# Grouped attention into a routed MoE: one transfer for a unit's q, one for its k, heads paired by two, five matmuls ahead of the first transposes, and q ahead of k in the first unit

## The chip, the cores and the metric

The kernel is one program on 1 core of a Trainium2 chip. The metric is device time in microseconds for one execution. A few runs are timed; their median stands for the kernel, and one further execution is taken with the hardware profiler, whose rows are quoted below.

## The reference

Attention is computed in chunks of 64 positions inside each head, with no mixing between chunks. Its output is the input of a mixture of experts in which a token keeps the expert of the token before it unless a gate says otherwise.

```python
B, H, S, D = 8, 8, 576, 64            # q, k, v: (B, H, S, D), float32
nc = S // 64
scores = scale * np.matmul(q_c, k_c.transpose(0, 1, 2, 4, 3))   # per 64-row chunk
attn = np.exp(scores - max); attn = attn / (sum + 1e-09)
out = np.matmul(attn, v_c)
...
x = out.transpose(0, 2, 1, 3).reshape(B, S, H * D)               # 512 columns, head after head
e = argmax(logits[b, s]) if s == 0 or local_gate[b, s] < 0.5 else prev_e
h = np.maximum(x[b, s] @ w1[e], 0.0)                             # 512 -> 1024
out[b, s] = p[e] * (h @ w2[e])                                   # 1024 -> 512
```

## The kernel before, in words

The 4608 rows (8 batches of 576) are cut into 18 units of 256 rows, numbered 0 to 17. A unit is 256 neighbouring rows of one batch, except units 6 and 15, whose rows are the last 64 of four batches ("mixed rows"). `load_qk(i)` fills two buffers of 512 KB, `qt` and `kt`, from a ring of six pairs (three of them are `lenth`/`lentl`, space that the weights take later). For a plain unit each of q and k comes in two transfers of 256 KB: partition 4p+g holds eight consecutive rows of head g in its first half (transfer j=0) and of head g+4 in its second half (j=1). For mixed rows each comes in four transfers of 128 KB. `load_v(i)` brings v, two transfers of 256 KB whose runs are 256 bytes long.

All transfers are issued from SyncE's queue (SP) in program order, the first unit's k excepted, which ScalarE's queue issues. There are eight completion semaphores for them, taken in turn, so a transfer waits for the one eight places ahead of it; SP also waits where the data queue takes no more.

A unit then passes these steps:
- `pair_heads`: four copies of 128x512 into `qr` and `kr` put heads side by side (`p0` = "AVPA" says which engines do it for unit 0: ScalarE, VectorE, GpSimd, ScalarE; later units all on GpSimd). Each copy reads both halves of `qt` or `kt`. `qr` and `kr` have one buffer each.
- `qk_transposes`: eight 128x128 transposes on TensorE for q and eight for k, in groups of four, each group copied out of PSUM to `qT` or `kT`.
- `scores`: 32 small matmuls into `sc`; row maxima, subtraction and exponential follow (`mx`, `pr`).
- `p_transposes`, then `values`: 32 matmuls with v into `o`, and a division by the row sum into `xs` (`norm`, one call for each half j of the heads).
- `x_transposes`, `router`: the logits; the unit's rows then go to `x_d` in DRAM.

The order on TensorE, VectorE, ScalarE and GpSimd is written out by hand: `PAR["start"]` for the first units (tokens such as `p0` pair, `t0a`..`t0d` the four groups of transposes, `s0` scores), `PAR["steady"]` for one iteration of the loop over units. In iteration i the loop handles scores of unit i+1, transposes of q and k of unit i+2, pairing of unit i+3, q and k loads of unit i+5 and v loads of unit i+2, beside the values of unit i-1 and the router of unit i-2. In the first unit four transposes of unit 1 (`t1a`) stand ahead of the scores of unit 0 (`s0`).

After the attention the rows are routed, gathered from `x_d` tile by tile and multiplied by the experts' weights; that is the rest of the program, and the change does not touch it.

The lines that set the heads' places in `values`, which stay for the units that are not changed:

```python
pT[64 * cc:64 * cc + 64, 4 * j + h, 64 * cp:64 * cp + 64],
vt[cp][64 * cc:64 * cc + 64, 4 * j + h, 0:D + 1],
```

Of the kernel before, what the change touches and what calls it, by code (L numbers as in the profile page):

```python
# [8 lines left out]
F32 = mybir.dt.float32  # L9
# [11 lines left out]
B, H, S, D = 8, 8, 576, 64  # L21
E, F = 8, 1024
C = H * D
N = B * S
P = 128
NT = N // P
NS = N // 256
# [50 lines left out]
def tile_attention_then_moe(ctx: ExitStack, tc, q, k, v, wg, wl, w1, w2, out):  # L78
    nc = tc.nc
# [7 lines left out]
    def ENG(x):  # L87
        return tuple({"A": nc.scalar, "V": nc.vector, "P": nc.gpsimd}[c] for c in x)

    ident = cpool.tile([P, P], F32, name="ident")  # L90
# [29 lines left out]
    ps_tr = ctx.enter_context(tc.tile_pool(name="ps_tr", bufs=3, space=PSUM))  # L120
# [7 lines left out]
    for i in range(2):  # L128
        vt = pa1.tile([P, VS], F32, name=f"v{i}")[:, 0:2 * H * DW].rearrange("p (c h d) -> p c h d", c=2, d=DW)
# [4 lines left out]
    def place(i):  # L134
        ph, j = divmod(i, 9)
        if j == LEFT:
            return 9 * ph + 8, [(4 * ph + n, 512, 64) for n in range(4)]
        j -= j > LEFT
        return 9 * ph + j, [(4 * ph + j // 2, 256 * (j % 2), 256)]

    def mixed_rows(i):
        return i % 9 == LEFT

    def load_qk(i):
        qt, kt = qkbuf[i % len(qkbuf)]
        for m, (b, s0, n) in enumerate(place(i)[1]):
            for dst, src in ((qt, q), (kt, k)):
                if mixed_rows(i):
                    nc.sync.dma_start(
                        dst[m::4].rearrange("p (h n) -> p h n", h=H),  # L150
                        src[b, :, s0:s0 + n, :].rearrange("h (p r) d -> p h (r d)", r=2))
                    continue
                for j in range(2):
                    (nc.scalar if i == 0 and src is k else nc.sync).dma_start(
                        dst[:, 8 * D * j:8 * D * j + 8 * D],
                        src[b, 4 * j:4 * j + 4, s0:s0 + n, :].rearrange("g (p r) d -> p g (r d)", r=8))
        return qt, kt
# [112 lines left out]
        return atoms  # L270


    def values(pT, vt, xs, fine=False):
        box = {}

        def group(j, h):
            if h == 0:
                box["o"] = ps_o.tile([P, 2, 512], F32, name="o")
            o = box["o"]
            for cp in range(2):  # L280
                for cc in range(2):
                    nc.tensor.matmul(
                        o[64 * cp:64 * cp + 64, cc, DV * h:DV * h + D + 1],
                        pT[64 * cc:64 * cc + 64, 4 * j + h, 64 * cp:64 * cp + 64],
                        vt[cp][64 * cc:64 * cc + 64, 4 * j + h, 0:D + 1],
                        start=True, stop=True,
                    )
            if h == 3 and not fine:
                norm(j)

        def norm(j):
                ov = box["o"][:, :, 0:4 * DV].rearrange("p c (h d) -> p c h d", d=DV)
                rs = pa2.tile([P, 2, 4], F32, name="rs")
                nc.vector.tensor_scalar_add(rs, ov[:, :, :, D], 1e-9)
                nc.vector.reciprocal(rs, rs)
                nc.vector.tensor_tensor(
                    xs[:, :, 256 * j:256 * j + 256].rearrange("p c (h d) -> p c h d", d=D),
                    ov[:, :, :, 0:D],
                    rs.unsqueeze(3).to_broadcast([P, 2, 4, D]),
                    ALU.mult,  # L300
                )

        out = []
        for j in range(2):
            out += [lambda j=j, h=h: group(j, h) for h in range(4)]
            if fine:
                out.append(lambda j=j: norm(j))
        return out
# [185 lines left out]
    qk, hd, vts, qkT, prs, pTs, xss, xTs = ({} for _ in range(8))  # L494

    def a_tq(i, engs=None):
        qkT[i] = (pe2.tile([P, 4, 256], F32, name="qT", bufs=1), pe2.tile([P, 4, 256], F32, name="kT", bufs=1))
        return qk_transposes(i, hd.pop(i), *qkT[i], engs)

    def a_pair(i, engs=(nc.gpsimd,) * 4):  # L500
        hd[i], fns = pair_heads(i, qk.pop(i), engs)
        return fns

    def a_sa(i, fine=False):
        prs[i] = pa2.tile([P, H, 2, D], F32, name="pr")
        return scores(*qkT.pop(i), prs[i], fine)

    def a_tp(i, fine=False):
        pTs[i] = pa2.tile([P, H, P], F32, name="pT")
        return p_transposes(prs.pop(i), pTs[i], fine)  # L510
# [3 lines left out]
    def a_va(i, fine=False):  # L514
        if not rows:
            rows.extend(pa2.tile([P, XS], F32, name=f"xs{n}", bufs=1) for n in range(NX))
        xss[i] = rows[i % NX][:, 0:2 * XR].rearrange("p (c n) -> p c n", c=2)
        if i < NX:
            nc.gpsimd.memset(xss[i][:, :, XL:XR], 0.0)
        return values(pTs.pop(i), vts.pop(i), xss[i], fine)  # L520

    def a_tx(i, fine=False):
        xTs[i] = pa2.tile([P, 4, 256], F32, name="xT", bufs=1)
# [5 lines left out]
    def play(order, qs):  # L529
        its = {}  # L530
        for tok in order.split():
            name, _, n = tok.partition("*")
            if name not in its:
                its[name] = iter(qs[name]())
            for _ in range(int(n or 1)):
                next(its[name])()
        for name, it in its.items():
            assert next(it, None) is None, name
        assert set(its) == set(qs), set(qs) - set(its)
# [54 lines left out]
    with tc.manual_schedule(engines=MAN | {ET.Pool}):  # L594
        warm = pa2.tile([P, 1], F32, name="warm", tag="xT", bufs=1)
        nc.scalar.activation(warm, ident[:, 0:1], AF.Exp)

        def load(store, fn, i):
            def go():
                store[i] = fn(i)  # L600
            return lambda: [go]

        tqs = {}

        def tq(i, g):
            if i not in tqs:
                tqs[i] = a_tq(i, ENG(PAR[f"t{i}"]))
            return tqs[i][5 * g:5 * g + 5]

        st = {f"p{i}": lambda i=i: a_pair(i, ENG(PAR[f"p{i}"])) for i in range(4)}  # L610
        st |= dict(
            s0=lambda: a_sa(0, True), q3=load(qk, load_qk, 3),
            s1=lambda: a_sa(1, True), o0=lambda: a_tp(0, True), q4=load(qk, load_qk, 4), q5=load(qk, load_qk, 5),
            v2=load(vts, load_v, 2))
        for i in range(3):
            for g in range(4):
                st[f"t{i}{'abcd'[g]}"] = lambda i=i, g=g: tq(i, g)
        st |= dict(wg=lambda: [lambda: (
            nc.sync.dma_start(wg9[:, :, 0:8], wg.rearrange("(c p) e -> p c e", p=P)),
            nc.sync.dma_start(wg9[:, :, 8:9], wl.rearrange("(c p) e -> p c e", p=P)))])  # L620
        play(PAR["start"], st)
# [247 lines left out]
    for i in range(1, NS - 2):  # L869
# [12 lines left out]
        if 8 <= i < 16:  # L882
            c, col = divmod(i - 8, 2)
# [13 lines left out]
    n = NS - 1  # L897
# [356 lines left out]
```

## Time and profile before

| | |
|---|---|
| median of 3 runs | 638.35 us (638.34 to 639.34) |
| profiled execution, its own time | 638.56 us |
| span from the first to the last instruction in it | 636.8 us |
| around the span | 1.76 us |
| TensorE (PE) busy | 608.1 us, 96% of the span |
| VectorE (DVE), ScalarE (ACT), GpSimd (POOL) busy | 380.3, 255.8, 147.0 us |
| moved by transfers | 97.83 MB, mean 154 GB/s |

A busy PE is not a PE at its peak: its matmuls are pipelined, their ends are modelled, and a pause of PE can lie inside a matmul's modelled time. All times within the execution count from the first instruction of the span. The first 160 us are the attention units, in which the transfers are dense; afterwards PE works on the experts.

### The profile page before, as it was taken

Reading aid. Unit: us, or ns where it says so; the run is one execution under the profiler, and the core shown is the slowest. Engines: PE = TensorE matmul, PEld = TensorE weight load, DVE = VectorE, ACT = ScalarE, POOL = GpSimd, SP = SyncE. Lnnn points to the kernel's source line nnn. Section 1 sums busy time; section 2 is a strip of 40 time slices with the busy share of each in tenths; the row PEclk is TensorE's granted clock in tenths of the full one; section 3 lists DMA queues with packets and bytes.
Section 4 is the critical chain, followed back from the end, with each engine's and each line's share of the span. In section 5 each row is a group of like instructions: output and inputs, shape, how many; then the busy total and the mean of one; then the engine's idle time right before and its main releaser. Section 6 shows DMA issues by size and latency. Waiting matters only on the chain. (4 is left out here: it accounts for less than half of the span.)

```text
span 636.8 us, 17170 instructions
## 1 busy us (share of the span) xinstructions
PE 608.1 (96%) x5904; PEld 513.6 (81%) x5904; DVE 380.3 (60%) x990; ACT 255.8 (40%) x468; POOL 147.0 (23%) x219
## 2 busy tenths in 40 slices
PE   4899989889999999999999999999999999999995
PEld 4788777777779788789998996789888998788884
DVE  2677678887795667575434556763478533387231
ACT  4677667664421252532112443421465211343120
POOL 3353244550050302021021021031021221010201
PEclk9999999999999999999999999999999999999999
DMA  8999999998440245155021264452086511054111
GB/s 267 264 265 301 284 272 264 303 286 271 158 150 21 71 151 185 44 178 180 20 70 55 61 206 134 151 178 64 27 271 203 190 52 59 30 184 147 65 30 36
DMA packets 78355, 97.83 MB, mean 154 GB/s; under 512 B 42672, under 2 KB 46768, under 8 KB 78192
## 3 DMA queue, kind: packets, MB, share of 16 engines
q1 hardware_dynamic: 71744, 75.30, 37.9%
q0 software_dynamic: 6160, 19.99, 9.6%
q8 instruction: 84, 1.38, 0.9%
q14 instruction: 79, 0.65, 0.3%
q10 hardware_dynamic: 288, 0.52, 0.3%
HBM read 76.62 MB, written 19.69 MB: 151 GB/s over the span
## 5 line engine op out<-in xcount | busy, mean ns | idle before, releaser
L804 POOL DMA_INDIRECT out<-ysb,sidx x38 | 40.2, 1058 | 356.3 <-DVEq L1028 160.6
L743 PE MATMUL y<-w2h,hq 128*128 128x512 f32 x368 | 119.8, 395 | 1.3 <-DVE ysb L1078 1.0
L743 PEld LDWEIGHTS y<-w2h,hq 128*128 128x128 f32 x368 | 69.1, 188 | 16.9 <-issue 2.5
L743 PE MATMUL y<-w2l,hq 128*128 128x512 f32 x184 | 71.9, 391 | 0.0
L1050 PE MATMUL tr<-xp,w1h 128*128 128x256 f32 x528 | 67.0, 283 | 0.0
L1050 PEld LDWEIGHTS tr<-xp,w1h 128*128 128x128 f32 x528 | 65.5, 192 | 1.2 <-ACT w2h L1011 0.4
L743 PE MATMUL y<-w2h,hp 128*128 128x512 f32 x192 | 63.3, 397 | 0.3 <-ACT hp L690 0.3
L722 PE MATMUL h<-w1h,xp 128*128 128x512 f32 x208 | 60.5, 396 | 0.0
L1058 ACT ACTIVATE hq<-tr 128x256 fp32r<-128x256 f32 x51 | 18.9, 383 | 68.4 <-PE tr L1050 44.8
L1078 DVE TENSOR_SCALAR ysb<-y,ppr 128x512 f32<-128x512 f32 x33 | 24.8, 751 | 34.4 <-PE y L743 30.3
L722 PEld LDWEIGHTS h<-w1h,xp 128*128 128x128 f32 x208 | 38.1, 188 | 7.4
L694 POOL DMA_INDIRECT xg<-x_d,gidx x36 | 38.5, 1069 | 19.8 <-issue 14.5
L743 PEld LDWEIGHTS y<-w2h,hp 128*128 128x128 f32 x192 | 36.0, 188 | 8.1 <-ACT hp L690 0.5
L789 ACT ACTIVATE hsb<-h 128x512 f32<-128x512 f32 x26 | 14.1, 596 | 66.1 <-PE h L722 49.1
L1059 DVE SCALAR_TENSOR_TENSOR hq<-tr,hq 128x256 fp32r<-128x256 f32 x51 | 21.1, 423 | 32.3 <-ACT hq L1058 28.6
L743 PEld LDWEIGHTS y<-w2l,hq 128*128 128x128 f32 x184 | 34.6, 188 | 6.9 <-DVEq L1028 0.3
L743 PE MATMUL y<-w2l,hp 128*128 128x512 f32 x96 | 37.5, 390 | 0.0
L1018 DVE TENSOR_TENSOR w1l<-raw,w1h 128x1024 fp32r<-128x1024 f32 x28 | 32.4, 1221 | 8.3 <-ACT w1h L1011 4.9
L691 DVE TENSOR_TENSOR xp<-tr,xp 128x512 fp32r<-128x512 f32 x39 | 25.5, 686 | 18.6 <-ACT xp L690 15.8
L1050 PE MATMUL tr<-xp,w1l 128*128 128x256 f32 x264 | 35.3, 283 | 0.0
L1018 DVE TENSOR_TENSOR w2l<-raw,w2h 128x1024 fp32r<-128x1024 f32 x28 | 32.8, 1223 | 1.2 <-issue 1.2
L1050 PEld LDWEIGHTS tr<-xp,w1l 128*128 128x128 f32 x264 | 33.3, 192 | 0.0
(242 smaller groups left out, 1152.7 us busy)
## 6 DMA issues: line engine op xcount, KB each, us to landing
raw<-in_moe_w SPq DMA_DIRECT2D x72, 512.0 KB
x_d<-xs SPq DMA_DIRECT2D x16, 528.0 KB
v<-in_v SPq DMA_DIRECT2D x20, 256.0 KB
qt<-in_q SPq DMA_DIRECT2D x16, 256.0 KB
lenth<-in_q SPq DMA_DIRECT2D x16, 256.0 KB
lentl<-in_k SPq DMA_DIRECT2D x16, 256.0 KB
kt<-in_k SPq DMA_DIRECT2D x14, 256.0 KB
raw<-in_v SPq DMA_DIRECT2D x6, 256.0 KB
```

Of the source, the lines that this page charges most:

```text
L691: lambda: V.tensor_tensor(lo, box["ps"], hi.bitcast(F32), ALU.subtract)]
L694: nc.gpsimd.indirect_dma_start(out=dst, out_offset=None, in_=src, in_offset=bass.IndirectOffsetOnAxis(ap=gidx[t].bitcast(U32), axis=0))
L722: nc.tensor.matmul(hs[:, j], xs[a][:, c], W1[w][c][:, 512 * j:512 * j + 512], start=(c == 0 and n == 0), stop=(c == 3 and n == 2))
L743: nc.tensor.matmul(y, h_of(t, f // 4)[a][:, f % 4], W2[w][c][:, f % 2, :], start=(f == 0 and n == 0), stop=(f == 7 and n == 2))
L789: nc.scalar.activation(hsb[:, 512 * j:512 * j + 512], hs[:, j], AF.Relu)
L804: nc.gpsimd.indirect_dma_start(out=out, out_offset=bass.IndirectOffsetOnAxis(ap=sidx[t].bitcast(U32), axis=0), in_=ysb, in_offset=None, bo ...
L1018: V.tensor_tensor(lo[c], raw[c], hi[c].bitcast(F32), ALU.subtract)
L1050: nc.tensor.matmul(hb[:, 256 * n:256 * n + 256], W1[w][c][:, P * (f + n):P * (f + n) + P], XP[:, x, c].rearrange("p s t -> p (s t)"), star ...
L1058: nc.scalar.activation(hi, ps, AF.Relu)
L1059: V.scalar_tensor_tensor(lo, ps, 0.0, hi.bitcast(F32), ALU.max, ALU.subtract)
L1078: V.tensor_scalar(ysb, y, pr, None, ALU.mult)
```

## The change

Four things are changed.

1. For units 1 to 15 without the mixed ones (13 units) q comes in one transfer of 512 KB and k in another. A partition then holds heads 2g and 2g+1 where it held g and g+4.
2. `values` follows: for those units head 2h+j of v goes with place 4j+h of the scores, and `norm` writes its half of the heads to every second block of 64 columns of `xs`.
3. In unit 0, SP and ScalarE's queue each issue one half of q first, and then one half of k.
4. Five matmuls on the identity matrix, 256 columns each, stand first on PE. Nothing reads their result.

```diff
+    def heads_by_two(i):
+        return 0 < i < NS - 2 and not mixed_rows(i)
...
+                if heads_by_two(i):
+                    nc.sync.dma_start(
+                        dst.rearrange("p (j n) -> p j n", j=2),
+                        src[b, :, s0:s0 + n, :].rearrange("h (p r) d -> p h (r d)", r=8))
+                    continue
                 for j in range(2):
-                    (nc.scalar if i == 0 and src is k else nc.sync).dma_start(
+                    (nc.scalar if i == 0 and j == 1 else nc.sync).dma_start(
...
+        if by_two:
+            xv = xs[:, :, 0:C].rearrange("p c (h j d) -> p j c h d", j=2, d=D)
+        else:
+            xv = xs[:, :, 0:C].rearrange("p c (j h d) -> p j c h d", j=2, d=D)
...
-                        vt[cp][64 * cc:64 * cc + 64, 4 * j + h, 0:D + 1],
+                        vt[cp][64 * cc:64 * cc + 64, 2 * h + j if by_two else 4 * j + h, 0:D + 1],
...
-                    xs[:, :, 256 * j:256 * j + 256].rearrange("p c (h d) -> p c h d", d=D),
+                    xv[:, j],
...
+        awake = ps_tr.tile([P, 4, P], F32, name="tr")
+        for _ in range(5):
+            nc.tensor.matmul(awake[:, 0:2], ident, ident.unsqueeze(1).to_broadcast([P, 2, P]), start=True, stop=True)
```

On SP's queue the program begins with these transfers before (`qt_120` and `kt_121` are unit 0's, the next two unit 1's, the next two unit 2's; `v_126` and `v_127` are v of units 0 and 1):

```order
L154 DMA qt_120<-in_q 128x1x512 x2
L154 DMA qt_122<-in_q 128x1x512 x2
L154 DMA kt_123<-in_k 128x1x512 x2
L165 DMA v_126<-in_v 128x8x64 x2
L154 DMA qt_124<-in_q 128x1x512 x2
L154 DMA kt_125<-in_k 128x1x512 x2
L165 DMA v_127<-in_v 128x8x64 x2
```

and with these of the change:

```order
L162 DMA qt_120<-in_q 128x1x512
L162 DMA kt_121<-in_k 128x1x512
L157 DMA qt_122<-in_q 128x2x512
L157 DMA kt_123<-in_k 128x2x512
L173 DMA v_126<-in_v 128x8x64 x2
L157 DMA qt_124<-in_q 128x2x512
L157 DMA kt_125<-in_k 128x2x512
L173 DMA v_127<-in_v 128x8x64 x2
```

From unit 1 on a pair of rows has become one row with twice the elements, and a half of unit 0's k has come in from ScalarE's queue, to which a half of its q went. On ScalarE's queue the start was this before (`warm` loads the exponential's table, `qr` and `kr` are the pairing copies):

```order
L154 DMA kt_121<-in_k 128x1x512 x2
L596 ACT_TABLE_LOAD
L596 ACTIVATE warm<-ident 128x1
L188 COPY qr<-qt_120 128x4x128
L188 COPY kr<-kt_121 128x4x128
```

and is this with the change:

```order
L162 DMA qt_120<-in_q 128x1x512
L162 DMA kt_121<-in_k 128x1x512
L608 ACT_TABLE_LOAD
L608 ACTIVATE warm<-ident 128x1
L196 COPY qr<-qt_120 128x4x128
L196 COPY kr<-kt_121 128x4x128
```

Only the two transfers differ. On PE the program begins so before (`tr<-ident,qr` are transposes of q, `sc` the scores of unit 0):

```order
L198 MATMUL tr<-ident,qr 128x128 x8
L198 MATMUL tr<-ident,kr 128x128 x8
L198 MATMUL tr<-ident,qr 128x128 x4
L233 MATMUL sc<-kT,qT 64x64 x32
L198 MATMUL tr<-ident,qr 128x128 x4
```

and so with the change:

```order
L611 MATMUL tr<-ident 128x256 x5
L206 MATMUL tr<-ident,qr 128x128 x8
L206 MATMUL tr<-ident,kr 128x128 x8
L206 MATMUL tr<-ident,qr 128x128 x4
L241 MATMUL sc<-kT,qT 64x64 x32
L206 MATMUL tr<-ident,qr 128x128 x4
```

The five matmuls stand ahead of all else; nothing behind them has moved.

## Rows read from the trace of the kernel before

**Rows 1.** The page: busy us of each engine, share of the span, instructions.
```profile
PE 608.1 (96%) x5904; PEld 513.6 (81%) x5904; DVE 380.3 (60%) x990; ACT 255.8 (40%) x468; POOL 147.0 (23%) x219
```

**Rows 2.** By the microsecond: busy us (instructions) by engine, granted clock, DMA share, GB/s.
```profile
2.00:3.00 1.00, 0.00 (x0) 0.00 (x0) 0.00 (x0) 0.94 (x1) 0.00 (x0) 1.00 0.59 131
3.00:4.00 1.00, 0.00 (x0) 0.00 (x0) 0.00 (x0) 0.55 (x2) 0.00 (x0) 1.00 1.04 354
4.00:5.00 1.00, 0.00 (x0) 0.00 (x0) 0.00 (x0) 0.00 (x0) 0.00 (x0) 1.00 1.07 412
5.00:6.00 1.00, 0.00 (x0) 0.00 (x0) 0.00 (x0) 0.00 (x0) 0.41 (x1) 1.00 1.02 393
6.00:7.00 1.00, 0.06 (x1) 0.09 (x2) 0.43 (x1) 0.82 (x2) 0.24 (x2) 1.00 1.06 404
```

**Rows 3.** Timeline from 0 to 40 us: start, duration, engine, line, operation, idle before.
```profile
1.43 0.28 POOL masks.py:199 TENSOR_SCALAR_AFFINE_SELECT ident<-ident 128x128 f32<-128x128 f32 x1
...
5.59 0.61 POOL L190 COPY kr<-kt 128x512 f32<-128x512 f32 x1 [3.87 <-DMA kt<-in_k]
...
6.18 0.62 ACT L188 COPY qr<-qt 128x512 f32<-128x512 f32 x1 [2.62 <-DMA qt<-in_q]
```

**Rows 4.** Timeline of PE from 5 to 32 us.
```profile
6.95 1.94 PE L198 MATMUL tr<-ident,qr 128*128 128x128 f32 x8 [6.95 <-ACT qr L188]
8.68 1.92 PE L198 MATMUL tr<-ident,kr 128*128 128x128 f32 x8
10.38 1.05 PE L198 MATMUL tr<-ident,qr 128*128 128x128 f32 x4
11.37 1.16 PE L233 MATMUL sc<-kT,qT 64*64 64x64 f32 x64
...
16.32 1.09 PE L198 MATMUL tr<-ident,qr 128*128 128x128 f32 x8
17.25 1.16 PE L198 MATMUL tr<-ident,pr 128*128 128x128 f32 x8
18.36 1.06 PE L198 MATMUL tr<-ident,kr 128*128 128x128 f32 x8
20.75 1.16 PE L233 MATMUL sc<-kT,qT 64*64 64x64 f32 x64 [1.33 <-ACT pr L252]
...
22.31 1.09 PE L198 MATMUL tr<-ident,qr 128*128 128x128 f32 x8
```

**Rows 5.** Timeline of PE around the first 512-column float32 matmuls in the experts.
```profile
257.12 3.65 PE L737 MATMUL m<-raw,fullx 128*64 128x512 f32 x16
```

**Rows 6.** Timeline from 0 to 40 us, GpSimd's pairing copies of units 2 and 3.
```profile
15.01 1.17 POOL L190 COPY kr<-kt 128x512 f32<-128x512 f32 x2 [0.60 <-DMA kt<-in_k]
...
18.96 1.17 POOL L190 COPY qr<-lenth 128x512 f32<-128x512 f32 x2 [2.78 <-DMA lenth<-in_q]
```

**Rows 7.** Waits of PE from 28 to 140 us: total us, times, longest.
```profile
PE sc L233 <- issue: 3.4, 5, 1.4
PE o L282 <- issue: 2.0, 2, 1.3
```

**Rows 8.** Timeline of PE from 40 to 80 us: the scores of unit 8.
```profile
64.89 0.58 PE L233 MATMUL sc<-kT,qT 64*64 64x64 f32 x24 [1.44 <-issue]
```

**Rows 9.** SP's timeline: k of unit 2, q of unit 3, v of unit 12.
```profile
9.22 1.25 SPq L154 DMA_DIRECT2D kt<-in_k  x2
...
12.06 3.34 SPq L154 DMA_DIRECT2D lenth<-in_q  x2
...
106.03 1.27 SPq L165 DMA_DIRECT2D v<-in_v  x2
```

**Rows 10.** Timeline of PE from 110 to 113 us: the values of unit 12.
```profile
111.87 0.65 PE L282 MATMUL o<-v,pT 64*64 64x65 f32 x32
```

**Rows 11.** Groups of VectorE from 0 to 150 us: line, op, count, busy us, mean ns.
```profile
L296 DVE TENSOR_TENSOR xs<-o,rs 128x512 f32<-128x512 f32 x33 | 22.8, 691 | 1.1
```

**Rows 12.** Transfer queues from 0 to 140 us: packets, MB, share.
```profile
q8 instruction: 22, 0.36, 1.0%
```

More of the change, by code (lines that the diff above doesn't have):

```diff
@@ L270, in p_transposes, with values @@
         return atoms
-    def values(pT, vt, xs, fine=False):
+    def values(pT, vt, xs, fine=False, by_two=False):
         box = {}
+        if by_two:
+            xv = xs[:, :, 0:C].rearrange("p c (h j d) -> p j c h d", j=2, d=D)
+        else:
+            xv = xs[:, :, 0:C].rearrange("p c (j h d) -> p j c h d", j=2, d=D)
         def group(j, h):
@@ L519, in a_va @@
             nc.gpsimd.memset(xss[i][:, :, XL:XR], 0.0)
-        return values(pTs.pop(i), vts.pop(i), xss[i], fine)
+        return values(pTs.pop(i), vts.pop(i), xss[i], fine, heads_by_two(i))
     def a_tx(i, fine=False):
```

## The prediction

> **What bounds the kernel now.** I read the page first, then the stretches, the timeline from the start, and last the waits. PE is busy for 608.1 us of the span of 636.8 [rows 1], so a gain must either start PE's work sooner or close one of its pauses. The chain that ended last does not reach back far enough to help: it covers only the tail of the program. So I follow PE from its first instruction. It does nothing for 6.95 us; its first transposes then wait for ScalarE's pairing copy of q [rows 4], and that copy was released by a transfer of q, at 6.18 [rows 3]. GpSimd's copy of k, released by k's transfers, started at 5.59 [rows 3]: k was there before q, though PE needs q first.
>
> The second thing is PE's speed. Eight transposes of q and eight of k run from 6.95 to 10.38 [rows 4], 0.214 us each. From 16.32 to 17.25 eight of the same shape take 0.93 us, 0.116 each [rows 4]. These are the two levels, 1.2 and 2.4 GHz. The granted clock reads 1.00 even in the stretch where PE starts [rows 2], so it has no record of the low level, and the spacing must tell. The slow spacing lasts until the scores at 11.37, which take 1.16 like later ones, at 20.75 for one [rows 4]: PE ran slow for 4.4 us after its first matmul and was at 2.4 GHz then.
>
> The third is who waits for transfers. After the first unit, rows say so only of GpSimd's copies: k of unit 2 at 15.01, q of unit 3 at 18.96 [rows 6], and a little for k of unit 3. PE's own pauses between 28 and 140 us are put down to "issue": 3.4 us before scores and 2.0 before values, in 7 pauses of up to 1.4 [rows 7]. So in the steady part the transfers are full but PE is fed; what is saved at the start should stay saved, as long as the transfers keep ahead.
>
> **The change, part by part.**
>
> *q ahead of k.* The data moved by 4.0 us is 131 + 354 = 0.485 MB; by 5.0 it is 0.897, by 6.0 1.290 and by 7.0 1.694 [rows 2]. The first pair of transfers (0.524 MB) is in at 4.1, the second (1.049 MB) at 5.4. Before, q's second half was the last of these four, and its copies began 0.8 after 5.4. With the change both halves of q are first on their queues, so its copies should begin at 4.1 + 0.8 = 4.9, 1.3 earlier; the copy on ScalarE takes 0.62 [rows 3], and q would be ready for PE at 5.65 (before, PE's 6.95 came 0.77 after 6.18). k is now last of the four: its copies begin at 6.2, 0.6 later than GpSimd's did, and with 0.62 each are done at 6.85. Unit 1's q is in when 1.573 MB have moved, 6.7, and can be copied from 7.5.
>
> *Five matmuls.* They need only the identity, which is done at 1.71 [rows 3], so they start near 1.8. No row shows this shape. The nearest are float32 matmuls of 512 columns, sixteen records side by side in pairs in 3.65 us [rows 5]: 0.43 to 0.46 for a pair at 2.4 GHz, so 0.22 for 256 columns, and a float32 matmul is two such records (the 32 of `scores` stand as x64 in a row). That is 0.44 each, 0.88 at 1.2 GHz: 4.4 us in all if slow, 2.2 if fast. PE is then free between 4.0 and 6.2. I take the slow end, since in the one stretch that tells, every matmul with less than 4.4 us of work behind it was slow. The first transposes then start at 6.2 instead of 6.95; the five matmuls cost about half a microsecond here, because q is ready at 5.65.
>
> *The clock.* 4.4 us after 1.8 is 6.2: if PE behaves as in its own first stretch, it is at 2.4 GHz when the transposes of q begin. They end at 7.15; those of k, ready at 6.85, follow until 8.1. Before, the scores started 0.99 after the end of k's transposes (8.68 to 10.38, then 11.37, with the copy to `kT` between) [rows 4]. With the change that gives 9.1. The four transposes of unit 1 that stand ahead of the scores need GpSimd's two copies, 1.17 [rows 6] from 7.5, so 8.67, and 0.47 of PE: 9.15. **Scores of unit 0 at 9.15 instead of 11.37: 2.2 us earlier.**
>
> *What the next units allow.* If their data comes no sooner than before, two places cap the gain. k of unit 2: GpSimd starts at 15.01, takes 1.17, and PE uses it at 18.36: 2.18 of slack. q of unit 3: 18.96 + 1.17 = 20.13 against 22.31: 2.18 again [rows 4, 6]. So 2.2 just fits.
>
> *One transfer for two.* Two transfers of 256 KB cost SP 1.25 us where it is not held up [rows 9]; one should cost half, since neither the bytes nor the runs (2 KB on the DRAM side) change. That frees 1.25 us of SP a unit. It hides behind the transfers themselves, which already move 354 to 412 GB/s from 3 us on [rows 2], and behind holds of SP like the 2.1 us in its 3.34 for q of unit 3 [rows 9], so I count 0. If the cover were gone, it would bring v, which stands behind k on SP, up to 1.25 us forward. A copy reads both halves of its buffer anyway, so nothing waits longer for a whole unit.
>
> *The heads' new places.* PE's matmuls only read other columns. `norm` writes blocks of 64 columns with gaps instead of 256 in a row, 13 units of 2 writes. They take 691 ns now [rows 11]. No row has the gapped form; from 0 to a doubling (0.7 us each) it would lie on VectorE, which is 60% busy, so 0 and no range of its own.
>
> The sum is made against the profiled execution: 638.56 - 2.2 = **636.4 us**. Its own time is 0.2 above the median of the runs, 638.35; I leave the number there. Differences under 0.2%, 1.3 us, are not told from no change here, so faster means under 637.1.
>
> **The rivals.**
>
> *The clock is late.* If the five matmuls don't bring PE to 2.4 GHz by the time the transposes start, or it falls back while only transposes run, 20 transposes cost 0.098 more each, 2.0 us; scores come near 10.9 and the gain is 0.5 (up to 1.2 if the clock comes in the middle). For: one stretch alone shows when it rises. Against: in that stretch nothing but transposes ran, and the scores that followed were fast. Time 637.8, chance 0.15. The Trainium skill has a rule of this kind: "TensorE: Matmul & The Clock Gate", Part 4, says that transposes do not count as work for the clock. By that rule the clock would not have risen before the scores at 11.37, and it had [rows 4]; so this trace does not bear it out.
>
> *The transfers set the pace later.* PE's lead of 2.2 us must be there at every unit. The tightest place I find is v of unit 12: SP has issued it by 107.30 [rows 9] and PE reads it at 111.87 [rows 10], 4.6 later. Where an engine did wait, the data came 4.5 after the end of the issue (k of unit 2: 10.47 to 15.01) and 3.6 (q of unit 3: 15.40 to 18.96) [rows 6, 9]. That leaves 0.1 to 1.0 us for v if SP keeps its times. It should not, having 1.25 us more a unit. If that helps nothing, the gain falls to about 1.0. Time 637.5, chance 0.15.
>
> *Slower, by the supply of instructions.* PE paused at 64.89 for 1.44 us in the middle of one group of 64 records [rows 8], where no data is waited for. Instruction packets, 22 in 140 us of 16 KB each [rows 12], share the transfer engines. Twice the bytes per request, issued sooner, may keep these engines fuller and such packets later. To turn the gain into a loss of 1.3 takes 3.5 us more: from 7 pauses [rows 7] to 10, at 1.2 each. At four more of 1.4: 636.4 + 5.6 = 642. For: the pauses exist only where transfers are dense. Against: the bytes are the same. The five matmuls also move the places where packets end by some twenty instructions, which can lose pauses as well as win them. Chance 0.10.
>
> *More than forecast.* The same shift takes away a pause or two (1.4 each), or the clock rises while the five matmuls run: 635.0. Chance 0.12.
>
> **How the numbers follow.** The forecast has 0.48: gains of 1.5 to 2.7, 635.9 to 637.0. Faster by over 0.2%: 0.48 + 0.12 + 0.03 of the two smaller gains = 0.63. Within 0.2%: 0.27. Slower: 0.10. For 8 in 10 I leave out the slower case and the better half of the best: 635.0 to 638.1.
>
> **What would show it.** In the profile after: copies of q on ScalarE and VectorE released by a transfer near 4.9 (right) or near 6 (q was not first in fact); PE's first row at 1.8, ending near 6.2; eight transposes of q in 0.93 us and not 1.7; scores of unit 0 near 9.15; q of unit 3 used near 20.1 on PE. Then the distance to the times of before should stay near 2.2 at 55, 110 and 160 us. If it shrinks with a wait on v, the transfers were the bound; if it jumps at rows with "issue", it was instructions. The forecast is wrong if the transposes stay slow, if a merged transfer lands later than its two halves did, or if pauses of PE change by more than 2 us in sum.

## The result, and the profile after

The changed kernel took 647.64 us (644.42 to 649.72, 4 runs) against 638.85 us (638.34 to 640.41, 4 runs) of the kernel before on the same chips: 1.0122 times as long, 95% interval 1.0097 to 1.0147. It is slower by 1.2%, about 8 us. Ratios in this text leave out executions more than 1.5% above the fastest of their kernel: two of late_merged (649.82 and 649.13), one each of after_again and merged_dummy. The forecast was 636.4, with 635.0 to 638.1 as its range; the case that came true was its rival of 0.10, the supply of instructions. A second measurement of the same kernel later gave 1.0101 (1.0066 to 1.0136).

The profiled execution took 644.42 us, with a span of 642.6, so it is one of the quicker ones. PE has 3.9 us more busy time than in [rows 1]; the five matmuls alone take 4.5:

```profile
PE 612.0 (95%) x5914; PEld 515.2 (80%) x5914; DVE 383.0 (60%) x990; ACT 255.8 (40%) x468; POOL 146.9 (23%) x219
```

**The start did most of what was forecast.** The timeline of the first 13 us (start, duration, engine, line, operation, idle before):

```profile
0.74 0.66 ACTq L162 DMA_DIRECT2D qt<-in_q  x1
...
1.77 4.54 PE L611 MATMUL tr<-ident 128*128 128x256 f32 x10 [1.77 <-POOL ident masks.py:199]
...
4.71 0.62 ACT L196 COPY qr<-qt 128x512 f32<-128x512 f32 x1 [1.14 <-DMA qt<-in_q]
...
6.16 1.04 PE L206 MATMUL tr<-ident,qr 128*128 128x128 f32 x8
...
7.03 1.23 PE L206 MATMUL tr<-ident,kr 128*128 128x128 f32 x8
...
8.86 1.16 POOL L198 COPY qr<-qt 128x512 f32<-128x512 f32 x2 [2.00 <-DMA qt<-in_q]
9.52 0.66 PE L206 MATMUL tr<-ident,qr 128*128 128x128 f32 x4 [1.26 <-POOL qr L198]
10.11 1.16 PE L241 MATMUL sc<-kT,qT 64*64 64x64 f32 x64
```

The copy of q starts at 4.71 (forecast 4.9). The five matmuls hold PE from 1.77 to 6.16. The eight transposes of q then take 0.87 us, from 6.16 to 7.03, where eight took 1.73 before [rows 4]: PE is at 2.4 GHz here, from the first transpose on (not so in every execution, see "Why the prediction was wrong"). But PE then waits 1.26 us for GpSimd's copy of unit 1's q, and that waited for its transfer: it can start at 8.86, not at 7.5. How much of this is the merging is not shown: the copy needs both halves in either form, and in the kernels with q first it starts between 7.55 (merged_dummy) and 9.50 us (no_awake) where unit 1's q is merged, between 7.34 (v_first_halves) and 8.37 (v_first_start) where it is not. The transfers as a sum are a little behind too (by the microsecond: busy us of PE, PEld, DVE, ACT, POOL, granted clock, DMA share, GB/s):

```profile
2.00:3.00 1.00, 1.00 (x3) 0.82 (x4) 0.00 (x0) 0.93 (x1) 0.00 (x0) 1.00 0.65 180
3.00:4.00 1.00, 1.00 (x3) 0.80 (x3) 0.00 (x0) 0.56 (x2) 0.00 (x0) 1.00 1.00 379
4.00:5.00 1.00, 1.00 (x4) 0.75 (x3) 0.28 (x1) 0.29 (x1) 0.00 (x0) 1.00 1.04 361
5.00:6.00 1.00, 1.00 (x4) 0.82 (x3) 0.15 (x1) 0.33 (x1) 0.00 (x0) 1.00 0.93 311
6.00:7.00 1.00, 1.00 (x9) 0.85 (x9) 0.21 (x1) 0.62 (x1) 0.66 (x2) 1.00 1.00 356
```

That is 1.59 MB by 7.0 where it was 1.69 [rows 2]. So the scores of unit 0 start at 10.11 instead of 11.37 [rows 4]: 1.26 us earlier, not 2.2. (Both are single executions: in v_first_before, whose start is that of the kernel before, these scores start at 12.50.)

**Then the lead turns into a loss.** The scores of unit 3 start 1.26 us earlier than before (25.11 for 26.37), those of unit 5 are level, those of unit 8 are 4.30 later (66.94 for 62.64), those of unit 17 5.30 later (140.93 for 135.63). From there to the end both kernels need about the same, 501.7 and 501.2 us. So 6.6 us are lost between unit 0 and unit 17. The waits of PE from 28 to 140 us (total us, times, longest), beside [rows 7]:

```profile
PE o L294 <- issue: 6.1, 6, 2.0
PE lg L345 <- DVE lT L341: 2.0, 2, 1.2
PE tr L448 <- DVE cinT L443: 1.5, 1, 1.5
PE lg L336 <- issue: 1.2, 1, 1.2
...
PE sc L241 <- issue: 0.4, 1, 0.4
PE lg L345 <- issue: 0.4, 1, 0.4
```

No transfer is among them. The waits for VectorE sum up to 3.9 us (0.4 of it in a row that is left out); the same view of the kernel before has 1.6. The larger part is "issue", the wait for nothing that the profile names, 8.1 us here and 6.1 in the same view of the kernel before (a row of 0.7 beside those of [rows 7]). In the trace the long ones (over 0.6 us from one record's start to the next) up to 125 us stand at record 961 of PE and PEld together, waits and branches of their sequencer counted in, and then 256 times 1, 3, 4, 5, 6, 8, 11 and 16 further on, to the record. In the kernel before four of the seven pauses in [rows 7] stand at such places; the other three, of 0.4 us each at 137 to 139 us, do not. A packet of the instruction queue has 16 KB, so 64 bytes a record if it holds 256: these are the places where PE has used up one packet and needs the next. The Trainium skill, "Advanced Engine Details and Errata", "Sequencer and Instruction Queues", says that a line of the instruction cache is 16 KB, 256 instructions; the trace agrees, with pauses at multiples of 256 records.

One such place in the timeline of PE:

```profile
52.98 0.33 PE L294 MATMUL o<-v,pT 64*64 64x65 f32 x5
55.27 0.68 PE L294 MATMUL o<-v,pT 64*64 64x65 f32 x27 [1.96 <-issue]
...
58.56 1.16 PE L241 MATMUL sc<-kT,qT 64*64 64x64 f32 x64
59.54 0.39 PE L294 MATMUL o<-v,pT 64*64 64x65 f32 x10
61.09 0.57 PE L294 MATMUL o<-v,pT 64*64 64x65 f32 x22 [1.15 <-issue]
```

PE stops after five of 32 matmuls of one group, whose data is there. The queues (packets, MB, share) of the stretch from 48.3 us, where PE went on after the packet end before, to 52.7:

```profile
q1 hardware_dynamic: 1207, 1.41, 103.2%
```

and of 52.7 to 54.1:

```profile
q1 hardware_dynamic: 1292, 0.33, 106.9%
q8 instruction: 1, 0.02, 5.7%
```

For 4.4 us only data moves. The packet runs from 52.76 to 54.04 and PE goes on at 55.27, 1.23 after its end. Up to 125 us every pause of this kind over 0.25 us ends 1.2 to 1.6 us after such a packet.

From this I take two numbers for each kernel, from the trace's records. The **wait** is the time from PE's going on after one packet end to the start of the next packet, as a mean of the 14 to 16 that lie between 20 and 110 us. The **pauses** are the sum of the times over 0.25 us from the start of one record of PE or PEld to the start of the next at packet ends, up to 147 us. Before: 2.4 and 6.5 us. After: 3.0 and 11.2. (As idle time of PE, without the modelled end of the matmul before, the same pauses are 4.7 and 8.2.) A wait of 3.0, one us for the packet and 1.4 behind it are 5.4 us, and PE needs only 4.3 for 256 short records (from 27.99 to 32.29 us in split_halves, described below). So 4.3 of the 6.6 us that are lost up to unit 17 lie at packet ends (10.8 before its scores, 6.5 in the kernel before), 3.5 if idle time is counted. The 2.3 us more of waits for VectorE are most of the rest; what they come from is not shown.

The new places of the heads cost nothing on VectorE, as forecast: the write is at 691 ns as in [rows 11] (line, op, count, busy us, mean ns).

```profile
L308 DVE TENSOR_TENSOR xs<-o,rs 128x512 f32<-128x512 f32 x32 | 22.1, 691 | 1.1
```

### The profile page after: what moved, and what is told of

It reads as the page before. It is cut to its first block, busy times and chain, and to the rows that moved or that the text cites. A ratio compares the mean times of both kernels' runs of the same rounds, so it can differ in the third digit from the quotient of the medians.

```text
span 642.6 us, 17140 instructions
## 1 busy us (share of the span) xinstructions
PE 612.0 (95%) x5914; PEld 515.2 (80%) x5914; DVE 383.0 (60%) x990; ACT 255.8 (40%) x468; POOL 146.9 (23%) x219
## 5 line engine op out<-in xcount | busy, mean ns | idle before, releaser
L709 POOL DMA_INDIRECT xg<-x_d,gidx x36 | 38.5, 1070 | 19.5 <-issue 13.8
```

The lines of the kernel that those rows point to most:

```text
L709: nc.gpsimd.indirect_dma_start(out=dst, out_offset=None, in_=src, in_offset=bass.IndirectOffsetOnAxis(ap=gidx[t].bitcast(U32), axis=0))
```

## The experiments

Each kernel was compared with the kernel before on one chip. "Wait", "pauses" and the scores of unit 17 are of one execution, whose own time stands behind them; the ratio is of 4 to 12.

| kernel | ratio, 95% interval | wait | pauses | unit 17 | that execution |
|---|---|---|---|---|---|
| before | 1 | 2.4 | 6.5 | 135.6 | 638.6 |
| changed | 1.0122, 1.0097 to 1.0147 | 3.0 | 11.2 | 140.9 | 644.4 |
| after_again | 1.0101, 1.0066 to 1.0136 | 3.3 | 13.8 | 143.2 | 647.4 |
| merged_only | 1.0110, 1.0081 to 1.0138 | 3.3 | 12.6 | 149.4 | 653.3 |
| no_awake | 1.0095, 1.0067 to 1.0123 | 3.2 | 10.7 | 142.4 | 645.4 |
| merged_xd_halves | 1.0075, 1.0043 to 1.0107 | 3.0 | 9.1 | 142.4 | 647.2 |
| q_merged | 1.0077, 1.0048 to 1.0107 | 2.8 | 7.2 | 138.8 | 641.3 |
| late_merged | 1.0028, 1.0002 to 1.0055 | 2.7 | 8.8 | 135.8 | 638.3 |
| merged_dummy | 1.0046, 1.0013 to 1.0079 | 2.5 | 3.9 | 133.4 | 638.0 |
| dummy_again | 1.0041, 1.0017 to 1.0064 | 2.8 | 9.0 | 136.3 | 640.9 |
| q_merged_xd_halves | 1.0062, 1.0036 to 1.0088 | 2.2 | 6.4 | 134.4 | 639.4 |
| split_halves | 0.9997, 0.9970 to 1.0025 | 2.1 | 2.8 | 136.4 | 641.4 |
| halves_again | 1.0014, 0.9993 to 1.0035 | 2.2 | 4.5 | 132.4 | 636.0 |
| start_only | 1.0012, 0.9990 to 1.0034 | 2.5 | 4.8 | 133.3 | 639.8 |
| start_again | 1.0003, 0.9975 to 1.0030 | 2.3 | 4.5 | 135.4 | 638.0 |
| xd_halves | 1.0057, 1.0028 to 1.0086 | 1.7 | 2.4 | 138.3 | 642.0 |

**1. Which part costs?** My theory was that the size of the transfers makes PE's instructions late. The rivals were the places where packets end, shifted by the five matmuls, and the heads' new places.

split_halves: the changed kernel with each merged transfer in two again, the heads where the change puts them.

```diff
-                    nc.sync.dma_start(
-                        dst.rearrange("p (j n) -> p j n", j=2),
-                        src[b, :, s0:s0 + n, :].rearrange("h (p r) d -> p h (r d)", r=8))
+                    for j in range(2):
+                        nc.sync.dma_start(
+                            dst[:, 8 * D * j:8 * D * j + 8 * D],
+                            src[b, j::2, s0:s0 + n, :].rearrange("g (p r) d -> p g (r d)", r=8))
```

> The changed kernel with each merged transfer issued as two of 256 KB again; the new places of the heads, the order of q and k at the start and the five matmuls stay, so PE runs the same program as in the changed kernel. Theory 'size' (a 512 KB transfer ahead of it makes PE's next 16 KB of instructions later): the 11.2 us of PE's stalls at packet ends up to 147 us fall back to some 6.7, the time is that of before less what the start gains: 635.5 to 637. Rival 'places' (the five matmuls shift where a packet ends in PE's program by 20 instructions, and packets now end where PE runs short instructions): PE's program is unchanged, so the stalls stay near 11 us and the time at 643 to 649. Rival 'heads' (the strided writes of the values cost VectorE and PE): 643 to 649 too, but with the lost time on VectorE's rows and not at packet ends.

merged_only: the changed kernel without the five matmuls and with the old order at the start; no_awake: without the five matmuls alone.

```diff
-        for _ in range(5):
-            nc.tensor.matmul(awake[:, 0:2], ident, ident.unsqueeze(1).to_broadcast([P, 2, P]), start=True, stop=True)
...
-                    (nc.scalar if i == 0 and j == 1 else nc.sync).dma_start(
+                    (nc.scalar if i == 0 and src is k else nc.sync).dma_start(
```

> The kernel before with the merged transfers and the new places of the heads alone: no five matmuls, q and k of unit 0 issued as before. Packets end where they ended before. Theory 'size': stalls of PE at packet ends of 9 to 12 us instead of 6.7, 641 to 647 us. Rival 'places': 638 to 639, stalls near 6.7. Rival 'heads': 641 to 647 with the loss on VectorE.

> The changed kernel without the five matmuls: q in front of k at the start, merged transfers. Theory 'size': as merged_only less at most 0.5 us for q, 641 to 647. Rival 'places': 637 to 639, since packets end where they did. Scores of unit 0 near 10.7 us (the transposes run at the low clock).

start_only: only the new start.

```diff
-        return 0 < i < NS - 2 and not mixed_rows(i)
+        return False
```

> The kernel before with the new start alone (q in front of k, five matmuls); all transfers of later units are 256 KB each and the heads stand as before. Scores of unit 0 near 9.2 us, since unit 1's q lands near 6.8 instead of 8.7. Theory 'size': 635.5 to 637. Rival 'places': 641 to 648, with stalls near 11 us at the same instruction numbers as in the changed kernel. Rival 'heads': 635.5 to 637.

The merged transfers alone cost 1.1%, with or without the rest. In halves, with PE's program unchanged to the instruction, the loss is gone. So "places" and "heads" are out, since both are still in split_halves. The waits of PE from 28 to 140 us in merged_only:

```profile
PE o L294 <- issue: 7.3, 5, 3.1
PE sc L241 <- issue: 3.3, 3, 1.5
```

and in split_halves:

```profile
PE lg L346 <- DVE lT L342: 2.5, 5, 0.8
PE sc L242 <- issue: 1.3, 3, 0.4
...
PE o L295 <- DVE xs L309: 1.0, 1, 1.0
PE o L295 <- DMA v<-in_v: 1.0, 3, 0.5
...
PE o L295 <- issue: 0.7, 1, 0.7
PE o L295 <- DMA raw<-in_v: 0.5, 1, 0.5
```

10.6 us of "issue" against 2.3, of which 0.3 stand at a transpose.

merged_only's execution, the slowest of its kernel, shows a second price of a late packet. Around its longest pause the granted clock falls to 0.50, that is 1.2 GHz (by stretch: us, busy us of PE, PEld, DVE, ACT, POOL, granted clock, DMA share, GB/s):

```profile
63.80:67.20 3.40, 3.25 (x25) 3.13 (x26) 2.43 (x6) 1.17 (x2) 0.00 (x0) 0.50 0.77 220
```

Eight transposes then take 1.76 us instead of 0.93 [rows 4]:

```profile
63.95 0.70 PE L294 MATMUL o<-v,pT 64*64 64x65 f32 x12 [3.07 <-issue]
64.58 1.97 PE L206 MATMUL tr<-ident,xs 128*128 128x128 f32 x8
66.34 1.47 PE L206 MATMUL tr<-ident,qr 128*128 128x128 f32 x8
```

The clock falls the same way near pauses of 1.88 and 1.82 us in q_merged (at 31.1 and 72.0 us), of 2.36 and 2.59 in merged_xd_halves (65.8, 96.5) and of 1.86 in q_merged_xd_halves (30.5), but not after each long one: the changed kernel's two profiles have pauses of 1.96 and 1.90 and no fall before PE's last matmul. They are slow all the same, so the clock is not the main cause. On the chips of merged_only, no_awake and after_again the mean granted clock (which counts the end of the program too) is 0.997 or more in 48 of 56 executions of the kernel before and in 7 of 28 of these three; those 7 are still 6.2 us slower than the 48.

The expected gain of the start is not there in the halves: 0.9997 and 1.0012 where 636 was expected. In split_halves transfers of v stand among PE's waits, which they did not before.

**2. Dose and place.** q_merged has q merged and k in halves; late_merged has merged transfers for units over 8 alone.

```diff
                 if heads_by_two(i):
+                    if src is q:
                         nc.sync.dma_start(
                             dst.rearrange("p (j n) -> p j n", j=2),
                             src[b, :, s0:s0 + n, :].rearrange("h (p r) d -> p h (r d)", r=8))
                         continue
+                    for j in range(2):
+                        nc.sync.dma_start(
+                            dst[:, 8 * D * j:8 * D * j + 8 * D],
+                            src[b, j::2, s0:s0 + n, :].rearrange("g (p r) d -> p g (r d)", r=8))
```

The edit of late_merged is the same with `if i > 8:` in place of `if src is q:`.

> The changed kernel with k in two transfers of 256 KB again and only q in one of 512 KB: half the dose. Theory 'size' (the size of a transfer sets how long PE's next instructions wait): the mean wait of an instruction packet between 20 and 110 us lies between 2.1 us (all in halves) and 3.0 (all merged), stalls at packet ends of 5 to 9 us, time 641 to 644. Rival 'threshold' (any merged transfer does it): as the changed kernel, 645 to 648. Rival 'k alone' (the second tensor in the queue is what hurts): 637 to 640.

> Merged transfers for units 9 to 15 alone, units 1 to 8 in halves. Theory 'size': PE's stalls follow the place: up to some 60 us (units up to 8 are then loaded) they are 1 to 3 us as in the kernel with all in halves, against 7 of the changed kernel; from 60 to 110 the packets' wait is near 3 us instead of 2.2. Time 640 to 644. Rival 'start' (what goes wrong is set by the first units): stalls as with all in halves everywhere, 636 to 639.

Half the dose costs between none and all: 1.0077, a wait of 2.8. In late_merged the loss follows the place: from 20 to 60 us the wait is 2.3 and the pauses 1.4 us, as in halves (2.1 and 0.0 in split_halves); from 60 to 110 it is 3.1 and 6.1, while split_halves has 2.1 and 1.3 there. The changed kernel has 3.5 and 7.0 in the first of these stretches. "Start" is out as a cause.

**3. Number or size?** Two things change with a merged transfer: it is larger, and SP, which needs as long for one as for the other (0.62 us for unit 1's q at 2.36, half the price of two), has sooner issued what follows, so that more is queued. merged_dummy puts a transfer of 64 bytes, which nobody reads, behind each merged one. That gives the number of the halves, with the size of the merged, and most of SP's pace: the small transfer takes SP 0.45 us as a median, a second half 0.60. It also takes one of the eight completion semaphores, as a second half does.

```diff
+                    nc.sync.dma_start(spare[next(turn) % 8], src[0, 0, 0:1, 0:16])
```

> The changed kernel with a transfer of 64 bytes, into a place that nobody reads, behind each merged transfer of units 1 to 15: as many transfers, and as much time of SP's, as with halves, but q and k still come in 512 KB each. If the size of a transfer holds the packets up: waits of 2.8 to 3.3 us between 20 and 110 us, stalls of 9 to 13 us, 644 to 648 us. If it is how far SP runs ahead: waits of 2.1 to 2.5, stalls of 3 to 6, 637 to 641.

> merged_dummy once more. If SP's pace makes most of it: 638 to 642, waits of 2.2 to 2.6. If the size of a transfer does: 642 to 646, waits of 2.8 to 3.2, and the first profile was a lucky one. If both have a part: 640.5 to 643.5 with waits between the changed kernel's and those of the halves.

> The changed kernel once more, for a second profile beside the two below. Packets wait 2.8 to 3.3 us between 20 and 110 us, stalls at packet ends of 9 to 13 us, 645 to 648 us.

> split_halves once more, the lower end: 637 to 640, waits of 2.0 to 2.4, stalls of 2 to 5 us.

The result lies between. Merged costs 1.0122 and 1.0101; with the small transfers 1.0046 and 1.0041; in halves 0.9997 and 1.0014. Of some 7 us between merged and halves about 4.3 go with SP's pace and the number of transfers. The other 2.4 may belong to the size, but that is not shown: the intervals of the last two pairs overlap, and the small transfer gives back only three quarters of a half's time on SP, so that in proportion 1.4 of the 2.4 could be pace too.

One quantity covers both: the data that SP and ScalarE's queue have issued and the transfer engines have not yet begun, by the records of the traces as a mean from 20 to 110 us. It is 0.52 to 0.61 MB in the kernel before and the five profiles with all loads in halves, 0.63 and 0.66 with the small transfers, 0.69 in q_merged, and 0.73 to 0.78 in the five with all merged. In the main the waits in the table rise with it, from 1.7 to 3.3 us, and 0.2 MB at the 273 GB/s of the kernel before are 0.7 us. That a packet waits behind more queued data is thus likely, whether the data is more transfers or larger ones; no run changes this quantity alone. The first execution profiled with the small transfers was the fastest of twelve; the second, at 640.9, has a wait between the two others, and its waits of PE from 28 to 140 us too:

```profile
PE o L299 <- issue: 3.8, 5, 1.0
PE sc L246 <- issue: 2.5, 5, 0.7
...
PE tr L211 <- issue: 1.0, 1, 1.0
```

**4. Smaller writes.** xd_halves has the new start alone, and each unit's write of 528 KB in two; the other two do the same in the changed kernel and in q_merged.

```diff
-                nc.sync.dma_start(xv[b, s0:s0 + n].rearrange("(c p) n -> p c n", p=P), xs)
+                for c in range(2):
+                    nc.sync.dma_start(xv[b, s0 + P * c:s0 + P * c + P], xs[:, c])
```

> The kernel before with the new start alone and, besides, each 528 KB write of a unit's rows to DRAM issued as two of 264 KB: the largest transfers that the kernel before has. Theory 'size', if it holds for writes too: packets wait less than 2.5 us between 20 and 110, stalls 2 to 4 us instead of 4.8, 634 to 637, faster than before. Rival 'loads only' (a write's pieces go out one by one with the loads and don't hold a packet up): 638 to 641 as the new start alone. Rival 'SP' (0.6 us more of issue for each unit makes data late): over 641, with PE waiting for GpSimd's copies.

> The changed kernel with each write of 528 KB in two of 264 KB. With the new start alone that brought the packets' wait from 2.3 to 1.7 us and the stalls from 4.5 to 2.4, and the loss came from data that landed late; here data lands 8 us early and SP has 1.25 us a unit to spare. By size: waits of 2.3 to 2.8, stalls of 6 to 9, 640 to 644. If the writes' size matters only where all else is small: as the changed kernel, 645 to 648.

> q in one transfer, k in two, each write in two: the issue time of SP is that of the kernel before. By size: waits of 2.0 to 2.5, stalls of 3 to 6, 637 to 641, below the 641.6 of q merged alone; if it beats the kernel before, below 637. If the writes' size doesn't matter: 641 to 643.

In xd_halves the wait falls to 1.7 and the pauses to 2.4, the least of all, and PE reaches unit 8 at 59.0 us, 3.6 earlier than before. Yet it is slower, 1.0057. From 28 to 140 us PE waits for no instructions at all in its list, but for others:

```profile
PE lg L345 <- DVE lT L341: 4.5, 4, 1.7
PE o L294 <- DVE xs L308: 1.1, 2, 0.7
PE o L294 <- DMA v<-in_v: 1.0, 3, 0.5
```

This is the rival "SP" of the expectation in part: what is late is v and VectorE's output, not GpSimd's copies. In the changed kernel the smaller writes left the wait at 3.0; the time went to 1.0075, within the intervals' reach of 1.0101. With q merged alone the waits fell from 2.8 to 2.2, and the time moved from 1.0077 to 1.0062, less than expected. So few packet waits alone don't make a fast kernel.

**5. Where the start's gain goes.** start_again is start_only once more.

> The new start alone once more, the same kernel as start_only: it was 641.1 us against 638.8, while its profile had scores of unit 17 at 133.3 us, 2.4 earlier than before. If the loss lies in the granted clock of one profiled execution (0.94 and 0.97 between 120 and 160 us), this profile will have its gain of some 2 us at unit 17 and at the end. If it lies in PE's stalls at packet ends, which vary from one execution to the next, their sum in this profile will differ by 1 us or more from 4.8. Time 637 to 642.

Both are level with the kernel before. In start_only's profile the lead at unit 17 is 2.4 us. 1.0 of it goes where the granted clock is 0.50, from 137.7 to 141.1 us, 0.8 more between 176 and 198 us at a clock of 1.00, and 1.8 in the tail, behind PE's last matmul. The tail is not the clock's doing: that matmul starts at 629.9 us and the clock falls at 632.6. What sets the tail is not shown. In start_again's the lead is 3.5 us at the scores of unit 12 (90.94 for 94.45) and 0.3 at unit 17, with the clock at 1.00 in between; from 155 us to the last matmul it is 1.4, and 0.6 at the end of the span. Its waits of PE from 28 to 140 us:

```profile
PE o L294 <- issue: 2.4, 3, 1.2
PE o L294 <- DMA lentl<-in_v: 1.5, 1, 1.5
```

Packet pauses were 4.5 us in it, against 4.8, so neither of the two guesses of the expectation holds for it: PE waited for a v that was late. By the trace's landing events v of units 7 to 11 comes at most 0.5 us ahead of PE there; in the kernel before it comes 2.4 to 4.0 ahead. It lands at about the same time in both (unit 9's at 84.7 and 84.6 us): PE had caught up with the transfers. halves_again shows the other end: it kept its lead, 132.4 at unit 17, and took 636.0 us, with the median of its runs at 640.35.

To test that v paces, the swap puts v of unit i+2 ahead of q and k of unit i+5 on SP, whose data waited 4 to 8 us:

```diff
-    "steady": "lq lv s*8 va*4 va s h0 tx*8 tq*8 s h1 va*4 ra*2 va h2 tq*8 ra*2 tp*8 s pr*4 h3 ",
+    "steady": "lv lq s*8 va*4 va s h0 tx*8 tq*8 s h1 va*4 ra*2 va h2 tq*8 ra*2 tp*8 s pr*4 h3 ",
```

> The new start alone, and in the steady loop v of unit i+2 issued ahead of q and k of unit i+5 instead of behind them. Theory 'v paces' (in the kernels without merged transfers the lead of the start is used up where v lands just when PE reads it: 0.0 to 0.9 us of slack for v of units 7 to 14, while q and k wait 4 to 8 us): v gets 2 to 4 us more slack, PE waits for no v, and the lead of some 2 us lasts to unit 17: 635 to 637.5. Rival 'packets alone' (only PE's stalls at packet ends count): the same transfers, stalls near 4.6, 638 to 641 as without the swap. Rival 'SP held' (v's buffers come free late, and q and k queue behind them): PE waits for GpSimd's copies of q and k, over 641.

> The changed kernel with the same swap, v ahead of q and k. There v lands 8 us and more before PE reads it, and the stalls at packet ends set the pace. Theory 'size': no gain, 644 to 648, stalls 9 to 13 us. Rival 'v paces everywhere': 638 to 642.

> All transfers in halves with the heads in their new places and the new start (split_halves), and v ahead of q and k. That kernel had the fewest stalls of those with the same issue (2.8 us) and v late by up to 0.9 us for units 6 to 11. Theory 'v paces': faster than before, 634 to 637. Rival 'packets alone': 638 to 639 as without the swap.

> The kernel before with the swap alone. v has 1.1 to 4.5 us of slack there and PE waits for none. Theory 'v paces': nothing to win in most executions, 637.5 to 639.5; a gain of a microsecond at most. If it gains over 2 us, more executions than the profiled one wait for v.

All four are slower: 1.0148 (1.0113 to 1.0183), 1.0164 (1.0129 to 1.0199), 1.0134 (1.0099 to 1.0169) and 1.0154 (1.0123 to 1.0185). v did come sooner against its use: 1.6 to 8.3 us ahead for units 5 to 14 of v_first_start. But SP's next instruction is the write of a finished unit, and it now queues behind 1 MB of q and k. VectorE's output buffers come free late, and PE waits for VectorE (5.6 us in 4 waits before its values, from 20 to 140 us in v_first_start). VectorE's waits from 20 to 140 us in v_first_start:

```profile
DVE xs L308 <- DMA x_d<-xs: 12.0, 7, 3.3
```

and in start_again:

```profile
DVE xs L308 <- DMA x_d<-xs: 1.7, 5, 0.4
```

None of my three theories named this wait. That v paces is thus shown by start_again's and split_halves' waits only, and the swap doesn't test it: it has put another late transfer in its place.

## Why the prediction was wrong

- **"One transfer for two … so I count 0" is the step that failed.** It looked at what SP's freed time could do for data, and put the bytes as unchanged. That is right for data: in the changed kernel v lands 7 to 12 us before its use at units 6 to 14. The bytes moved between 20 and 110 us tell nothing: 25.0 to 26.2 MB in the five profiles with all merged, 24.2 to 25.9 in those with halves. What it missed is who else uses the transfer engines. PE's instructions come through them, 22 packets in 140 us [rows 12], and they came 0.6 to 1.0 us later each. That term is about 7 us (merged_only 1.0110), not 0.
- **The rival "slower, by the supply of instructions" had the mechanism**, with "twice the bytes per request, issued sooner, may keep these engines fuller and such packets later", and a price of 642. The profiled execution took 644.4, the median 647.6; up to unit 17 the pauses at packet ends grew by 4.3 us, where 5.6 was the guess for four more. "The bytes are the same" was counted against it, and the pauses that were already there [rows 7] counted too little for it: four of those seven stand at packet ends, so the supply was late at some of them before. "PE is fed" was a misreading for the same reason: PE waited for no data there, but for instructions.
- **The start** was forecast at 2.2 us and gave 1.26 at unit 0, because unit 1's q was copied at 8.86 and not at 7.5. In halves it was copied at 8.02 to 8.35 and the start gave 1.7 to 2.1 (scores of unit 0 at 9.71, 9.57, 9.27 and 9.60). q first and the length of the five matmuls behaved as in the forecast. The clock did so in the changed kernel's profile, and there by luck: the 4.4 us between PE's first matmul and the high level were one reading. In the sixteen profiles with the five matmuls the spacing of PE's records halves (0.43 to 0.22 us among the five, 0.21 to 0.11 among transposes) somewhere between 5.1 and 7.9 us; in ten of them some or all of the first eight transposes still run at 1.2 GHz, in start_only all eight:

```profile
6.20 1.91 PE L206 MATMUL tr<-ident,qr 128*128 128x128 f32 x8
7.91 1.09 PE L206 MATMUL tr<-ident,kr 128*128 128x128 f32 x8
```

There they take 1.71 us, 0.8 more than at the high level, so the clock rival is not out; it cost less than its 2.0 us, since PE was at the high level for the transposes of k. In no_awake, without the five, PE's first scores still take 1.99 us at 11.21, at the low level, 5.6 us after its first matmul.

- **"What is saved at the start should stay saved"** failed as well. Without merging no gain of the start can be measured (0.9997 to 1.0014, with intervals of some 0.25% to either side, so 1 us is not excluded). The rival "the transfers set the pace" named the place, v of the units around 12 (in start_again it is late at units 9 and 10), and its gain of 1.0 is within the intervals.
- The five matmuls' shift of packet ends, feared and hoped for in two rivals, is not seen: start_only has pauses of 4.8, the kernel before 6.5, no_awake and the changed kernel 10.7 and 11.2.

The Trainium skill, "DMA: Bandwidth & Descriptors", "Rules for kernel authors", asks for 1 MiB and more per transfer for the highest bandwidth. By that rule merging would help here. The traces show no clear gain in bytes moved (25.0 to 26.2 MB from 20 to 110 us merged, 24.2 to 25.9 in halves), and the time says the contrary.

What stays open: in what order the transfer engines take instruction packets among data, and whether the size of a transfer has a part of its own beside the amount that is queued. Nor is it shown for each execution why the same kernel differs by 6 to 8 us from run to run (halves_again from 635.96 to 642.11); of the three ways seen, late packets, late v and falls of the granted clock, a profile shows only its own.

## What to carry to other kernels

Where PE runs hundreds of short instructions in a few microseconds beside full transfer queues, look for "issue" pauses at places a multiple of 256 records apart, each just behind an instruction packet: they say that the instructions themselves are late, and then queueing more data ahead of them can cost PE time though the bytes are the same. Before a saving on an issuing engine is counted as 0, ask what that engine will do with the time. And a lead of PE is worth only what the next bound leaves of it: here v landed 1 to 4 us ahead of its use at units 7 to 14, and a gain of 2 us had met it by the middle of the kernel.

## What was not expected of the hardware

- Instruction packets of 16 KB start 2.1 to 2.5 us after PE has begun on the one before, with transfers of 256 KB in the queues, and 3.0 to 3.3 with 512 KB; with the writes at 264 KB too, 1.7 (xd_halves). A packet takes 1.0 to 1.2 us as a mean, and PE goes on about 1.4 after its end.
- A transfer of 64 bytes cost SP 0.44 to 0.69 us (median 0.45), three quarters of the 0.61 of one of 512 KB, and one behind each merged transfer made the changed kernel faster by 0.6 to 0.8%.
- Near a pause of PE of 1.8 to 3.1 us the granted clock can fall to 0.50 (63.8 to 67.2 us in merged_only; also in q_merged and merged_xd_halves), so that a late packet is paid for twice; it does not always.
- The clock's rise at the start came between 5.1 and 7.9 us in sixteen profiles with the same five matmuls, begun at 1.77 or 1.78.
- Runs of one kernel on one chip spread by 8 to 9 us: 634.93 to 642.61 for 28 of the kernel before, 640.77 to 649.43 for 10 of the changed one.
